# Dilated v blocks of 72 and 108 rows in a fused attention and gated unit kernel

## The chip, the cores and the metric

The kernel runs on one core of a Trainium2 chip. The metric is the time of one execution on the device in microseconds (us), as the median of several runs. A core has five engines that run side by side: TensorE (PE, matmuls and transposes into PSUM), VectorE (DVE), ScalarE (ACT), GpSimd (POOL) and SyncE (SP), which here issues the transfers. The transfers themselves are carried by 16 DMA engines[...].

## The reference, cut to what matters

Eight batches of eight heads, 576 positions, head size 64. Heads 0 to 3 use a plain window of 32 keys, heads 4 to 7 a dilated one: 32 keys at a distance of 4. The result goes through a causal convolution of 5 taps, a sigmoid gate and two 512 x 512 matmuls.

```python
rel = pos[:, None] - pos[None, :]
mask_plain = (rel >= 0) & (rel < window)                       # window = 32
mask_dil = (rel >= 0) & (rel < window * dilation) & (rel % dilation == 0)   # dilation = 4
...
attn = softmax(scale * q @ k.T, masked)      # heads 0-3 plain, heads 4-7 dilated
x = (attn @ v).transpose(0, 2, 1, 3).reshape(B, S, H * D)
...
gate_pre += conv_w[k] * xp[:, k:k + S, :]    # k = 0..4
gate = 1.0 / (1.0 + np.exp(-gate_pre))
out = (gate * (x @ w_val)) @ w_out
```

In the dilated heads a query at position 4t + r sees only keys at positions 4t' + r. The kernel therefore splits the 576 positions into four residues r with 144 places t each (TT), and a query at t sees keys t - 31 to t.

## The kernel before, in words

The work comes in 16 units: for each batch one unit of the four dilated heads and one of the four plain heads. For each unit, SP loads q and k (576 KB each) and v. TensorE transposes q and k into PSUM (line 431), DVE and ACT copy them to SBUF (lines 292 and 294), TensorE makes the scores (line 450), ACT takes the exponential (line 470), DVE multiplies by the mask (line 476), and TensorE multiplies with v (line 487 for dilated, 514 for plain heads). DVE divides by the sum (lines 497 and 526). After both units of a batch come the transposes of the result (lines 535 and 551), the convolution (line 569), the gate and the two big matmuls (lines 584 and 600), and the stores (line 614).

Of a plain unit, q and k pass through a cast on POOL (line 294, tiles qc and kc) before TensorE can transpose them; of a dilated unit they are transposed as loaded (tiles qn and kn). All v goes through a cast on POOL, from `va` to `vd` for dilated heads and from `vp` to `vpb` for plain ones.

The dilated v of a batch is cut into two blocks for the two halves of the queries, t = 0 to 71 (z = 0) and t = 72 to 143 (z = 1). Queries of the first half need keys 0 to 71, those of the second half keys 41 to 143. `KB` (line 219) is the number of partitions of each block's tile, 80 and 128. Block 1 puts key t on partition t - T1, with T1 = TT - 128 = 16. Its lowest partitions hold keys that no query of this half sees, so they are not loaded: `Z1` (line 221) is the first partition that is loaded, 16, and the partitions below it are set to zero once, at the start (line 364, on DVE). So block 0 loads keys 0 to 79 (80 rows, 320 KB), block 1 keys 32 to 143 (112 rows, 448 KB). A row is the four residues of one place t, that is 1 KB from each of four heads.

The matmul of line 487 uses `et[0:KB[z]]` and all KB[z] partitions of `vd`. The mask makes the weights of keys outside the window zero.

The order of the work is set before the program is built. A planner (`Plan`) holds a list of tasks with dependencies, costs and a due time (`KEY`), and places them on the engines; the tasks are then written out in the order of their planned starts. Loads all lie on SP's queue, one after the other, in the order of the units: for a dilated unit q, k, v block 0, v block 1, for a plain unit q, k, v half 0, v half 1. The planner's cost for the two dilated v loads is written out as 1.25 and 1.75. Every load waits until the tile that it writes has been read for the last time: there are two buffers each of va and vp, three of qn and kn, and three of vd and vpb. In the first 20 us, where the plan finds TensorE idle, it puts warm matmuls (line 627) whose result nobody reads.

The lines of the loads:

```python
rows = v[b, 4:8].rearrange("h (p r) d -> p h (r d)", r=R)
if z == 0:
    nc.sync.dma_start(out=vas[z][n % 2], in_=rows[0:KB[0]])             # line 401
else:
    nc.sync.dma_start(out=vas[z][n % 2][Z1:KB[1]], in_=rows[T1 + Z1:TT])  # line 403
```

Of the kernel before, what the change touches and what calls it, by code (L numbers as in the profile page):

```python
# [197 lines left out]
def kernel(  # L198
# [17 lines left out]
    W = 32  # L216
    TT = S // R
    QB = TT // 2
    KB = (80, 128)
    T1 = TT - KB[1]  # L220
    Z1 = 16
    JP, JD = 9, 18
    scale = 1.0 / float(D) ** 0.5
    NCH = Dm // 128
# [22 lines left out]
    vps = [consts.tile([128, 4 * NG, 2, D], FP32, name=f"vp{i}") for i in range(2)]  # L247
    vas = [[consts.tile([KB[z], 4, R * D], FP32, name=f"va{z}{i}") for i in range(2)]
           for z in range(2)]
    vds = [[consts.tile([KB[z], 2, R, DA], BF16, name=f"vd{z}{i}") for i in range(NVD)]  # L250
           for z in range(2)]
# [58 lines left out]
    def const(name, eng, dur, emit, deps=(), key=-50):  # L310
        return plan.add(name, key, {eng: (dur, dur + 0.05)}, lambda t: emit(), deps,
                        port=("POOL",))
# [42 lines left out]
    def dve_consts():  # L355
# [7 lines left out]
        for x in vas[1]:  # L363
            nc.vector.memset(x[0:Z1], 0.0)
    c_dv = const("dve_consts", "DVE", 2.2, dve_consts, key=-59)
# [31 lines left out]
    def load_vd(u, n, z):  # L397
        b = units[u][0]
        rows = v[b, 4:8].rearrange("h (p r) d -> p h (r d)", r=R)
        if z == 0:  # L400
            nc.sync.dma_start(out=vas[z][n % 2], in_=rows[0:KB[0]])
        else:
            nc.sync.dma_start(out=vas[z][n % 2][Z1:KB[1]], in_=rows[T1 + Z1:TT])

# [74 lines left out]
    def attn_d(t, sc, i, hf):  # L479
# [3 lines left out]
        for z in range(2):  # L483
            for x in range(2):
                for hh in range(2):
                    c = 2 * z + hh
                    nc.tensor.matmul(out=ps[:, x * 512 + c * DA:x * 512 + (c + 1) * DA],  # L487
                                     lhsT=et[0:KB[z], x, c * QB:c * QB + 128],
                                     rhs=vds[z][n][:, hh, 2 * hf + x, :],
# [396 lines left out]
```

## Time and profile before

| what | value |
|---|---|
| time, median of 3 runs | 193.21 us (190.97 to 197.29) |
| span of the profiled run | 191.4 us |
| mean granted TensorE clock | 0.988 |
| transfers | 43.41 MB, of these read from HBM 33.56 MB |

The busy shares of the engines are shares of the span. The row of tenths cuts the span into 40 slices of 4.8 us; a 9 means that the 16 DMA engines were busy 90% or more of the slice on the mean. The page's section on DMA issues gives each kind of transfer with its count, its size and the median time from issue to landing:

```profile
qn<-in_q_dram SPq DMA_DIRECT2D x16, 576.0 KB, 9.8
kn<-in_k_dram SPq DMA_DIRECT2D x16, 576.0 KB, 11.3
vp<-in_v_dram SPq DMA_DIRECT2D x15, 384.0 KB, 11.4
va<-in_v_dram SPq DMA_DIRECT2D x8, 448.0 KB, 9.9
va<-in_v_dram SPq DMA_DIRECT2D x8, 320.0 KB, 7.1
```

A landing time of about 10 us for a load of half a megabyte is mostly time spent queued behind earlier loads. In the list of groups a row gives line, engine and operation, the tiles and shapes, the count, then busy time and mean duration, then the idle time of the engine before them and what ended it. In a timeline, a row is start, length, engine, line, operation, tiles, count, and in brackets the idle time before it and who ended it.

### The profile page before, as it was taken

How to read it: one execution, taken by the hardware profiler on the slowest of the kernel's cores; microseconds unless marked ns; L12 is line 12 of the kernel's file. 1: busy time of each engine (PE TensorE's matmuls, PEld its weight loads, DVE VectorE, ACT ScalarE, POOL GpSimd, SP SyncE). 2: the span in 40 equal slices, each digit the busy share in tenths (PEclk: the TensorE clock that was granted, in tenths of full speed). 3: DMA queues.
4: the chain of work that ended last, by engine and by line, in shares of the span. 5: the costliest groups of instructions: out<-in, count | busy, mean ns of one | idle time of the engine just before them, and what ended most of it. 6: DMA issues, size and time to landing. Idle time of an engine off the chain costs nothing.

```text
span 191.4 us, 6733 instructions
## 1 busy us (share of the span) xinstructions
PE 166.2 (87%) x2892; PEld 113.2 (59%) x2892; DVE 128.4 (67%) x239; ACT 123.0 (64%) x204; POOL 61.7 (32%) x99
## 2 busy tenths in 40 slices
PE   7999988788888779989896998989999989999890
PEld 2546456655676547766673765655675876757540
DVE  7498585967576858667877576997667978930500
ACT  2448976575796839768845577775786394658151
POOL 7964308236332552803632207351007000000000
PEclk9999999999999999999999699999999999999998
DMA  5999999999999999999999839996451312035256
GB/s 199 269 384 235 379 255 288 234 264 278 232 341 335 252 290 233 366 294 303 296 210 269 245 115 259 361 246 247 169 172 52 113 58 110 3 104 160 68 169 215
DMA packets 32102, 43.41 MB, mean 227 GB/s; under 512 B 1877, under 2 KB 20293, under 8 KB 32074
## 3 DMA queue, kind: packets, MB, share of 16 engines
q1 hardware_dynamic: 32064, 42.99, 81.3%
q8 instruction: 22, 0.36, 0.9%
q14 instruction: 6, 0.05, 0.1%
q10 hardware_dynamic: 10, 0.01, 0.1%
HBM read 33.56 MB, written 9.44 MB: 225 GB/s over the span
## 4 chain that ended last, share of the span: by engine, by line
PE 57%; DVE 12%; ACT 11%; DMA 9%; issue 6%; POOL 1%; ACTq 0%; SPq 0%; DVEq 0%
PE ps L600 14%; PE ps L584 13%; DMA kn<-in_k_dram 8%; PE ps L569 7%; PE ps L627 6%; PE ps L431 5%; PE ps L450 4%; ACT et L470 4%; PE ps L487 3%; ACT osb L605 3%; DVE et L476 3%; PE ps L514 2%; PE ps L535 2%; DVE qT L294 2%; ACT qT L292 2%
## 5 line engine op out<-in xcount | busy, mean ns | idle before, releaser
L470 ACT ACTIVATE et<-ps 128x576 bf16<-128x576 f32 x64 | 40.6, 653 | 17.4 <-PE ps L450 17.2
L584 PE MATMUL ps<-xT,w_val 128*128 128x288 bf16 x256 | 36.0, 286 | 3.5 <-issue 2.2
L600 PE MATMUL ps<-w_out,gy 128*128 128x512 bf16 x144 | 35.7, 380 | 2.9 <-ACT osb L605 1.9
L593 DVE SCALAR_TENSOR_TENSOR gy<-gy,ps 128x576 bf16<-128x576 bf16 x32 | 23.9, 750 | 14.9 <-PE ps L584 14.7
L605 ACT ACTIVATE osb<-ps 128x512 f32<-128x512 f32 x35 | 20.0, 598 | 18.9 <-PE ps L600 17.0
L294 POOL CAST vd<-va 80x512 bf16<-80x512 f32 (+1 forms) x32 | 20.7, 678 | 33.1 <-DMA va<-in_v_dram 14.2
L584 PEld LDWEIGHTS <-w_val 128*128 128x128 bf16 x256 | 23.7, 98 | 11.2 <-issue 5.6
L569 PE MATMUL ps<-xT,diag 64*64 64x288 bf16 x640 | 25.1, 287 | 2.4 <-issue 0.7
L294 POOL CAST vpb<-vp 128x768 bf16<-128x768 f32 x16 | 13.5, 863 | 38.6 <-DMA vp<-in_v_dram 21.7
L476 DVE TENSOR_TENSOR et<-et,mask_p 128x576 bf16<-128x576 bf16 x32 | 18.7, 591 | 7.0 <-ACT et L470 6.3
L476 DVE TENSOR_TENSOR et<-et,mask_d 128x576 bf16<-128x576 bf16 x32 | 20.2, 636 | 4.3 <-ACT et L470 3.9
L497 DVE TENSOR_TENSOR xnd<-ps,rec 72x512 bf16<-72x512 f32 x32 | 22.0, 687 | 1.1
L600 PEld LDWEIGHTS <-gy 128*128 128x128 bf16 x144 | 12.7, 98 | 15.6 <-issue 3.1
L577 ACT ACTIVATE gy<-ps 128x576 bf16<-128x576 f32 x32 | 20.2, 658 | 2.7 <-PE ps L569 2.5
L569 PEld LDWEIGHTS <-diag 64*64 64x64 bf16 x640 | 18.0, 107 | 5.3 <-issue 3.4
L292 ACT COPY xT<-ps 128x576 bf16<-128x576 bf16 (+1 forms) x20 | 15.7, 786 | 7.2 <-PE ps L551 3.7
L292 ACT COPY qT<-ps 128x576 bf16<-128x576 bf16 x22 | 13.6, 643 | 10.5 <-PE ps L431 7.8
L450 PE MATMUL ps<-qT,kT 64*64 64x96 bf16 (+1 forms) x640 | 18.6, 203 | 1.6 <-ACT kT L292 1.0
L450 PEld LDWEIGHTS <-kT 64*64 64x64 bf16 (+1 forms) x640 | 12.4, 102 | 12.3 <-issue 8.1
L627 PE MATMUL ps<-warm 128*128 128x512 bf16 x52 | 15.7, 429 | 1.3 <-DVE warm L314 1.3
L292 ACT COPY kT<-ps 128x576 bf16<-128x576 bf16 x21 | 12.9, 644 | 4.6 <-PE ps L431 2.7
L526 DVE TENSOR_TENSOR xnp<-ps,den 96x768 bf16<-96x768 f32 x16 | 15.3, 954 | 0.5
(68 smaller groups left out, 181.1 us busy)
## 6 DMA issues: line engine op xcount, KB each, us to landing
qn<-in_q_dram SPq DMA_DIRECT2D x16, 576.0 KB, 9.8
kn<-in_k_dram SPq DMA_DIRECT2D x16, 576.0 KB, 11.3
out_dram<-osb SPq DMA_DIRECT2D x24, 256.0 KB, 2.6
vp<-in_v_dram SPq DMA_DIRECT2D x15, 384.0 KB, 11.4
va<-in_v_dram SPq DMA_DIRECT2D x8, 448.0 KB, 9.9
va<-in_v_dram SPq DMA_DIRECT2D x8, 320.0 KB, 7.1
out_dram<-osb SPq DMA_DIRECT2D x8, 192.0 KB, 2.4
wst<-in_moe_w_val_dram SPq DMA_DIRECT2D x2, 512.0 KB, 8.4
```

What stands on the lines that cost most here:

```text
L292: nc.scalar.copy(out=dst, in_=src)
L294: op(t.eng).tensor_copy(dst, src)
L450: nc.tensor.matmul(out=ps[po:po + pn, x, out_c:out_c + ln], lhsT=kw[rb, k0:k0 + (pn - 1) * kstep + 1:kstep], rhs=qT[rb, q0:q0 + (ln - 1) * ...
L470: nc.scalar.activation(out=ets[(2 * i + hf) % NE][:, :, 0:HALF], in_=ps[:, :, 0:HALF], func=AF.Exp, scale=scale)
L476: op(t.eng).tensor_tensor(out=ev, in0=ev, in1=m.to_broadcast([128, 2, HALF]), op=ALU.mult)
L497: nc.vector.tensor_tensor(out=xnd[i % 2][:, 4 * hf:4 * hf + 4].rearrange("p (x j) h d -> p x (j h) d", x=2), in0=av[:, :, :, 0:D], in1=rec ...
L569: nc.tensor.matmul(out=ps[o:o + 64, 512 * f:512 * f + HALF], lhsT=diag[lo:lo + 64, c * K + kk, :], rhs=xT[lo:lo + 64, b % NX, c, f * HALF ...
L584: nc.tensor.matmul(out=ps[:, 512 * f:512 * f + HALF], lhsT=w_val[f][:, mc, c * 128:(c + 1) * 128], rhs=xT[:, b % NX, mc, K - 1 + f * HALF: ...
L593: nc.vector.scalar_tensor_tensor(out=y, in0=y, scalar=1.0, in1=ps[:, :, 0:HALF], op0=ALU.add, op1=ALU.mult)
L600: nc.tensor.matmul(out=ps, lhsT=y[:, c, 128 * n:128 * n + 128], rhs=w_out[f][:, c, :], start=(c == 0), stop=(c == NCH - 1))
L605: nc.scalar.activation(out=osb[z % NO], in_=bank(ou), func=AF.Copy, scale=0.5)
L627: plan.idle = lambda t: nc.tensor.matmul(out=bank(t), lhsT=warm[:, 0:128], rhs=warm, start=True, stop=True)
```

## The change

Block 0 gets a tile of 72 partitions instead of 80 and loads keys 0 to 71, exactly those that its queries see. Block 1 is loaded from partition 20 on instead of 16, that is keys 36 to 143; partitions 0 to 19 are zeroed at the start. The two loads of a batch shrink from 320 and 448 KB to 288 and 432 KB. The casts of block 0, the memsets of its column of ones and the matmuls of line 487 for z = 0 go over 72 partitions instead of 80. The aim is not to load rows that no query uses. The order of the instructions on every engine is the same as before.

```diff
-    KB = (80, 128)
+    KB = (72, 128)
     T1 = TT - KB[1]
-    Z1 = 16
+    Z1 = 20
```

## The prediction

> **What bounds the kernel now.** I read the busy slices first, then the DMA queues, then the order in time of the loads, of the casts on POOL and of TensorE's transposes, because the diff touches loads alone. From the page:
>
> ```profile
> span 191.4 us, 6733 instructions
> PE 166.2 (87%) x2892; PEld 113.2 (59%) x2892; DVE 128.4 (67%) x239; ACT 123.0 (64%) x204; POOL 61.7 (32%) x99
> DMA  5999999999999999999999839996451312035256
> DMA packets 32102, 43.41 MB, mean 227 GB/s; under 512 B 1877, under 2 KB 20293, under 8 KB 32074
> q10 hardware_dynamic: 10, 0.01, 0.1%
> ```
>
> TensorE is the busiest engine, but the DMA row is at 9 from the second slice to the 23rd (a slice is 4.8 us, so from 5 to 110 us). Both look like a bound; the question is who waits for whom, and when. The timeline of POOL's casts, and beside it that of TensorE:
>
> ```profile
> 10.29 2.28 POOL L294 CAST vd<-va 80x512 bf16<-80x512 f32 x4
> 28.97 1.18 POOL L294 CAST vd<-va 80x512 bf16<-80x512 f32 x2 [7.22 <-DMA va<-in_v_dram]
> 30.76 1.40 POOL L294 CAST vd<-va 128x512 bf16<-128x512 f32 x2 [0.61 <-DMA va<-in_v_dram]
> 35.37 1.15 POOL L294 CAST kc<-kn 128x1152 bf16<-128x1152 f32 x1 [1.90 <-DMA kn<-in_k_dram]
> 50.59 1.15 POOL L294 CAST kc<-kn 128x1152 bf16<-128x1152 f32 x1 [1.99 <-DMA kn<-in_k_dram]
> 67.00 1.15 POOL L294 CAST kc<-kn 128x1152 bf16<-128x1152 f32 x1 [1.72 <-DMA kn<-in_k_dram]
> ```
> ```profile
> 27.76 0.62 PE L431 MATMUL ps<-ident_b,kn 128*128 128x128 bf16 x8 [0.73 <-DMA kn<-in_k_dram]
> 36.58 0.68 PE L431 MATMUL ps<-ident_b,kc 128*128 128x128 bf16 x9 [1.05 <-POOL kc L294]
> 52.29 0.66 PE L431 MATMUL ps<-ident_b,kc 128*128 128x128 bf16 x9 [0.73 <-ACT qT L292]
> 74.11 0.66 PE L431 MATMUL ps<-ident_b,kc 128*128 128x128 bf16 x9
> ```
>
> The reader is to see the slack between a load and TensorE's use of it (start plus length of the cast, against the start of the transposes). At 27.76 TensorE starts when kn lands: slack 0. At 36.58 it starts 0.06 us after the cast that began at 35.37: slack 0. At 52.29 the cast has been done since 51.74: slack 0.55. At 74.11 the cast has been done since 68.15: slack 6.0. So up to about 52 us the loads set TensorE's pace; after that TensorE falls behind the loads and they have room to spare, although the DMA row still shows 9. The chain of waits says the same: its only long DMA step is kn, and none of the loads appears on it after 36 us.
>
> [...] conv_nat has 5 rows, and its queue q10 shows 10 packets, 5 rows and 5 completions. The page lists 117 issues on SP; 117 x 16 + 5 = 1877, which is exactly the count under 512 B. So every load from SP now uses 16 engines. [...] The trace does not show single engines. [...] Between 22 and 24 us, where 128-row k is loaded, DMA moves 409 GB/s; between 16 and 18, where the 64-row halves of vp are loaded, 231; in the v stretch:
>
> ```profile
> GB/s 237 310 218 319 182 510 182 182 182 300 218 164 164 200 182 146 319 146 164 200 200 237 246 200 182 219 109 182 219 209 218 218 237 127 200 164 182 218 237 218
> DMA packets 454, 0.48 MB, mean 214 GB/s; under 512 B 17, under 2 KB 448, under 8 KB 453
> ```
>
> (window 24.75 to 27.00 us).
>
> **The change part by part.** Rows: (80 - 72) + (112 - 108) = 12 rows of 4 KB fewer per head group, 48 KB; over 8 pairs of loads 0.39 of 43.41 MB. At the 214 GB/s above that would be 0.22 us less per pair, if nothing else changed.
>
> Engines: [...] both loads go from 16 engines to 12. A row is four pieces of 1 KB (one per head). Per engine, before: 80 x 4 / 16 + 112 x 4 / 16 = 20 + 28 = 48 pieces; after, on twelve: 72 x 4 / 12 + 108 x 4 / 12 = 24 + 36 = 60, on the other four none. Twelve engines get 12 pieces more per pair. Price of a piece: in the v stretch 431 pieces (448 less 17 completions) on 16 engines in 2.25 us make 84 ns each[...]. The lower end is from the stretch 12 to 14 us, where 340 pieces of 2304 B make 2 x 16 / 340 = 94 ns each, 24.5 GB/s per engine, hence an estimate of 42 ns for 1 KB. So 12 pieces cost 0.5 to 1.0 us. I take 0.8 to 1.0[...]. The pair takes about 3.0 us now (from kn at 27.76 to the cast of the second block at 30.76).
>
> Who feels it: the loads form one stream on SP's queue, with qp, kp, vp, qd, kd behind each pair, so each pair makes all later loads that much later. At 27.76 one pair lies ahead (its casts ran at 10.29): +0.8 to 1.0. At 36.58 two: +1.6 to 2.0. At 52.29 three: +2.4 to 3.0, less the slack of 0.55, so TensorE is 1.9 to 2.5 us late, of which 1.6 to 2.0 were already there. Later pairs cost nothing: by 67 us four pairs make 3.2 to 4.0 us of lag, TensorE is itself some 2 us late, and 2 us are taken from a slack of 6. TensorE's order is fixed and it is 87% busy, so the 2 us are not won back. Sum: +1.9 to +2.5 us, middle 2.2; 193.2 + 2.2 = 195.4.
>
> Costed at nothing: POOL's casts, 668 ns with 80 rows and 688 with 128, so rows are not what they cost; the attention matmuls, 195 ns with 80 rows and 193 with 128; the two memsets of 16 or 20 rows on DVE, 912 ns each, which take as long on more partitions and run at 3 to 5 us while TensorE issues warm matmuls. No wait and no instruction is added, and the planner's costs for these loads (1.25 and 1.75) are constants, so the order on every engine stays.
>
> **The rivals.**
> (a) [...] engines don't matter[...]. Against: 60 pieces at even the unhindered 42 ns are 2.5 us, so twelve engines cannot do better than that, and the measured 3.0 leaves room only if waits shrink. With three pairs saving up to 0.22 us each: 192.6 to 193.2.
> (b) Worse. The twelve engines stay out of step with the four, which run ahead into the next transfers; these land only when the last engine is done[...]. With a lag of 1.5 to 2.2 us per pair: 3 x 1.5 - 0.55 = 4.0 to 3 x 2.2 - 0.55 = 6.1 us, so 197 to 199.5. For it: load stretches already fall from 409 to about 210 GB/s. [...]
> (c) Fewer engines than twelve[...]: 8 and 4 would give 36 + 108 = 144 pieces per engine, at 42 ns 6.0 us per pair, 3 more than now; 3 x 3 - 0.55 = 8.5, and 201.7 or more. [...]
> (d) Faster. The loads give back what TensorE waits for them at 27.76 and 36.58, 1.8 us: 191.4. It needs the v loads to become shorter by more than the 48 KB.
>
> **How the numbers follow.** Forecast 0.52, (a) 0.15, (b) 0.25, (c) 0.04, (d) 0.04. The bound of 2% is 3.9 us, 197.1. Slower: (b), (c) and a fifth of the forecast for spread between runs (190.97 to 197.29 before): 0.39. Faster over 2% needs more than (d) gives, with spread: 0.06. The rest, 0.55, is within 2%. The range runs from (a) to the top of (b): 192.8 to 199.8.
>
> **What would show it.** Engines: under 512 B must read 101 x 16 + 16 x 12 + 5 = 1813, and packets in all 32102 - 384 - 64 = 31654; 1877 would mean that 16 engines are still used and the engine step is wrong. Lag: kc's casts now at 35.37 and 50.59 should start 1.6 to 2.0 and 2.4 to 3.0 us later, and TensorE's wait before them should grow. The cast at 67.00 should move too without TensorE waiting for it. If the casts have moved and the end has not, TensorE won the time back[...]. A wait for va or kn behind TensorE after 60 us would mean that the slack of 6 us was spent, and (b).

## The result, and the profile after

The changed kernel takes 200.35 us (median of 4 runs, 199.81 to 202.28); the kernel before took 193.33 us beside it (190.97 to 197.29). The ratio is 1.0423 with a 95% interval of 1.0297 to 1.0550: slower, by about 7 us, three times the 2.2 us that were forecast and above the range. Ratios here and below are of the runs within 1.5% of the fastest run of their kernel; where none is given, too few of those were left or only one run was made, and the times stand by themselves.

The head of the page of the kernel after, with the row of granted clock:

```profile
span 198.7 us, 6733 instructions
PE 169.3 (85%) x2892; PEld 114.3 (58%) x2892; DVE 128.8 (65%) x239; ACT 122.6 (62%) x204; POOL 60.9 (31%) x99
...
PEclk9999999969988996999999999999999999999998
DMA  6999999999999999999999999999976211115256
...
DMA packets 31654, 43.02 MB, mean 217 GB/s; under 512 B 1813, under 2 KB 19845, under 8 KB 31626
```

The same instructions as before, and 0.39 MB less to move. The DMA row is at 9 up to the 29th slice (144 us) where it was at 9 up to the 23rd (110 us): fewer bytes, and the DMA engines are busy with them for longer. Under 512 B stands 1813 and the packets are 31654, the two counts that the prediction named for twelve engines.

When the loads land is seen in the timeline of POOL, in the casts of the plain unit's k (start, length, tiles, and in brackets POOL's idle time before it and who ended it):

```profile
18.50 1.15 POOL L294 CAST kc<-kn 128x1152 bf16<-128x1152 f32 x1 [2.21 <-DMA kn<-in_k_dram]
...
38.17 1.15 POOL L294 CAST kc<-kn 128x1152 bf16<-128x1152 f32 x1 [1.69 <-DMA kn<-in_k_dram]
...
56.64 1.15 POOL L294 CAST kc<-kn 128x1152 bf16<-128x1152 f32 x1 [2.75 <-DMA kn<-in_k_dram]
...
76.15 1.15 POOL L294 CAST kc<-kn 128x1152 bf16<-128x1152 f32 x1 [2.10 <-DMA kn<-in_k_dram]
...
114.28 1.15 POOL L294 CAST kc<-kn 128x1152 bf16<-128x1152 f32 x1 [2.29 <-DMA kn<-in_k_dram]
```

Before, these five began at 16.64, 35.37, 50.59, 67.00 and 98.47 us, and the one between the last two at 80.26 (after: 92.30). The first and the last of them, before:

```profile
16.64 1.15 POOL L294 CAST kc<-kn 128x1152 bf16<-128x1152 f32 x1 [1.34 <-DMA kn<-in_k_dram]
...
98.47 1.15 POOL L294 CAST kc<-kn 128x1152 bf16<-128x1152 f32 x1 [2.19 <-DMA kn<-in_k_dram]
```

The lag is 1.86, 2.80, 6.05, 9.15, 12.04 and 15.81 us: six pairs of loads, 2.6 us for each on the mean. TensorE's transposes of the same tile, from its timeline:

```profile
39.38 0.68 PE L431 MATMUL ps<-ident_b,kc 128*128 128x128 bf16 x9 [1.92 <-POOL kc L294]
...
57.84 1.14 PE L431 MATMUL ps<-ident_b,kc 128*128 128x128 bf16 x9 [2.36 <-POOL kc L294]
...
82.38 0.66 PE L431 MATMUL ps<-ident_b,kc 128*128 128x128 bf16 x9
...
120.90 0.66 PE L431 MATMUL ps<-ident_b,kc 128*128 128x128 bf16 x9
```

These were at 36.58, 52.29, 74.11 and 112.73 before. The last of them, before:

```profile
112.73 0.66 PE L431 MATMUL ps<-ident_b,kc 128*128 128x128 bf16 x9
```

TensorE is 2.80, 5.55, 8.27 and 8.17 us later, and 7.3 at the end of the span. At the first two the cast has just ended and TensorE was idle for it, 1.92 and 2.36 us (1.05 us before the first of them in the kernel before, and before the second it waited for ACT). At the last two there is no bracket: TensorE did not wait, though the casts were 9 and 15.8 us late. So the loads set the pace up to 58 us, which explains 5.55 of the 7.3 us. The last 1.8 us came later, and not from a wait for a load: between the second and the third of these transposes TensorE loses another 2.7 us, part of which it wins back by the end. In that stretch the clock is granted at half for 3.4 us twice, at 57.7 (which is why nine transposes took 1.14 us at 57.84) and at 74.8; an earlier such stretch is at 40.6. And one idle time that no record explains, ahead of line 584, is 3.56 us (at 74.72) where it was 2.23 before (at 68.01). These two were not told apart. The stretch at 74.8 begins right behind the idle time of 3.56 us; near the first two, TensorE's waits last 1.92 and 2.36 us. What sets off such a stretch was not shown.

The DMA engines' share and the bytes moved, in two windows of 20 us of each kernel (columns: window, length, busy time and count of PE, PEld, DVE, ACT, POOL, granted clock, DMA share, GB/s). Before:

```profile
20.00:40.00 20.00, 16.45 (x317) 11.36 (x307) 14.09 (x25) 13.84 (x23) 7.91 (x10) 1.00 1.09 296
40.00:60.00 20.00, 17.34 (x366) 12.27 (x367) 14.61 (x30) 15.10 (x25) 8.19 (x11) 1.00 1.09 286
```

After:

```profile
20.00:40.00 20.00, 15.97 (x300) 10.69 (x299) 13.35 (x22) 13.30 (x22) 6.66 (x8) 1.00 1.06 267
40.00:60.00 20.00, 16.45 (x284) 11.09 (x284) 11.90 (x22) 13.10 (x22) 6.47 (x8) 0.86 1.06 227
```

The DMA share stays above 1 (the records of pieces overlap) while GB/s falls from 286 to 227. So the queues hold work all the time, and each piece takes longer: over the whole trace the mean record of a 2304-byte piece (the plain units' q and k, queued right behind the v pair) grew from 121 to 149 ns, of a 4608-byte piece (the dilated q and k) from 243 to 262, while the 1 KB pieces of the v pair itself went only from 67 to 68. The pieces that slowed down are not those of the changed loads but their neighbours'.

The trace also holds the time at which each DMA engine reports the end of its part of a load, one end for each engine (no view prints these): 16 for each load of q, twelve for each changed load of v beside one record at its issue. For the plain q of the second batch, issued at 20.37 us right behind the v pair, the first four of 16 ends come from 27.15 to 27.83 us and the other twelve from 33.52 to 35.27. So four engines are 5.7 us ahead of the rest: they have finished even the first half of the plain v, two loads further on, at 33.13. In the kernel before, the 16 ends of the same q lie between 29.93 and 32.09, and no two neighbours are as much as 1 us apart. Whether this lead is the cause, is what the experiments ask.

### The profile page after: what moved, and what is told of

It reads as the page before. It is cut to its first block, busy times and chain, and to the rows that moved or that the text cites. A ratio compares the mean times of both kernels' runs of the same rounds, so it can differ in the third digit from the quotient of the medians.

```text
span 198.7 us, 6733 instructions
## 1 busy us (share of the span) xinstructions
PE 169.3 (85%) x2892; PEld 114.3 (58%) x2892; DVE 128.8 (65%) x239; ACT 122.6 (62%) x204; POOL 60.9 (31%) x99
## 2 busy tenths in 40 slices
DMA packets 31654, 43.02 MB, mean 217 GB/s; under 512 B 1813, under 2 KB 19845, under 8 KB 31626
## 4 chain that ended last, share of the span: by engine, by line
PE 46%; DMA 24%; ACT 10%; DVE 7%; issue 6%; SPq 2%; POOL 2%; ACTq 0%; DVEq 0%
DMA kn<-in_k_dram 23%; PE ps L584 14%; PE ps L600 12%; PE ps L569 5%; PE ps L431 4%; PE ps L450 4%; ACT osb L605 3%; ACT et L470 3%; PE ps L514 2%; PE ps L487 2%; PE ps L535 2%; DVE et L476 2%; DVE qT L294 2%; POOL kc L294 2%; ACT kT L292 2%
## 5 line engine op out<-in xcount | busy, mean ns | idle before, releaser
L470 ACT ACTIVATE et<-ps 128x576 bf16<-128x576 f32 x64 | 40.6, 653 | 22.0 <-PE ps L450 21.7
L584 PE MATMUL ps<-xT,w_val 128*128 128x288 bf16 x256 | 38.2, 297 | 4.4 <-issue 3.6
L584 PEld LDWEIGHTS <-w_val 128*128 128x128 bf16 x256 | 24.5, 101 | 13.2 <-issue 6.5
L294 POOL CAST vd<-va 72x512 bf16<-72x512 f32 (+1 forms) x32 | 20.0, 652 | 37.6 <-DMA va<-in_v_dram 36.1
L627 PE MATMUL ps<-warm 128*128 128x512 bf16 x52 | 16.2, 438 | 1.3 <-DVE warm L314 1.3
```

The lines of the kernel that those rows point to most:

```text
L294: op(t.eng).tensor_copy(dst, src)
L470: nc.scalar.activation(out=ets[(2 * i + hf) % NE][:, :, 0:HALF], in_=ps[:, :, 0:HALF], func=AF.Exp, scale=scale)
L584: nc.tensor.matmul(out=ps[:, 512 * f:512 * f + HALF], lhsT=w_val[f][:, mc, c * 128:(c + 1) * 128], rhs=xT[:, b % NX, mc, K - 1 + f * HALF: ...
```

## The experiments

Four theories. A: the twelve engines simply have more to do (60 pieces for 48 in each pair). B: the four engines without a share run ahead into later transfers, so that pieces of different transfers meet and slow each other. C: it is the rows themselves (72 and 108, or where they start). D: the harm is done inside the pair, beside the q and k in flight at its start.

**Same rows, nearly all engines (e1_split).** Each load is cut into a part that divides by 16 and a remainder.

```diff
-    KB = (80, 128)
+    KB = (72, 128)
-    Z1 = 16
+    Z1 = 20
-            nc.sync.dma_start(out=vas[z][n % 2], in_=rows[0:KB[0]])
+            nc.sync.dma_start(out=vas[z][n % 2][0:64], in_=rows[0:64])
+            nc.sync.dma_start(out=vas[z][n % 2][64:72], in_=rows[64:72])
-            nc.sync.dma_start(out=vas[z][n % 2][Z1:KB[1]], in_=rows[T1 + Z1:TT])
+            nc.sync.dma_start(out=vas[z][n % 2][32:128], in_=rows[T1 + 32:TT])
+            nc.sync.dma_start(out=vas[z][n % 2][20:32], in_=rows[T1 + 20:T1 + 32])
```

> The rows of the change (72 and 108), but block 0 loaded as 64 + 8 rows and block 1 as 96 + 12, so that most rows go over all 16 engines: at most 48 pieces of 1 KB per engine and pair of loads, as before, at least 40; 16 transfers more in all. Theory A (the transfer waits for its busiest engine: the twelve engines have 60 pieces instead of 48): back to 193 to 194.5 us, and the casts of kc at 35 and 51 us again. Theory B (engines that get no share of the pair run ahead[...]): nearly back as well, 193.5 to 195, since the shares differ by 8 pieces and not by 60. Theory C (it is the rows: casts, memsets, matmuls on 72 rows, or where block 1 begins): stays at 199 to 202.

Measured: 188.63 us (188.09 to 189.50) beside 192.72 of the kernel before, ratio 0.9842 (0.9755 to 0.9929). POOL's timeline of it:

```profile
35.79 1.15 POOL L294 CAST kc<-kn 128x1152 bf16<-128x1152 f32 x1 [2.57 <-DMA kn<-in_k_dram]
51.89 1.36 POOL L294 CAST kc<-kn 128x1152 bf16<-128x1152 f32 x1 [2.66 <-DMA kn<-in_k_dram]
```

The second and third cast are back within 0.4 and 1.3 us of where they were before, and the loss is gone. Under 512 B stands 2037, 160 more than before: 52 for each batch, which fits parts of 64, 8, 96 and 12 rows on 16, 8, 16 and 12 engines, where the two loads of before had 32. The bytes, the partitions and the matmuls over 72 partitions are those of the changed kernel, so C falls: the loss does not come from the rows. (Whether it is truly faster than before is taken up below.)

**One engine without a share instead of four (e2_k15).** Blocks of 75 and 105 rows on fifteen engines (the count is below): 20 + 28 = 48 pieces for each, as many as sixteen got before.

```diff
-    KB = (80, 128)
+    KB = (75, 128)
-    Z1 = 16
+    Z1 = 23
```

> Blocks of 75 and 105 rows (second block from partition 23), both multiples of 15: 75 x 4 / 15 + 105 x 4 / 15 = 20 + 28 = 48 pieces on 15 engines, none on the sixteenth. Theory A: the busiest engine has the 48 pieces of before, so 193 to 194.5 us. Theory B: one engine of 16 runs ahead by 48 pieces per pair, so something between, 194.5 to 198. If the rows alone mattered (C), near the 200 of the change, as both blocks are within 3 rows of it.

Measured: 191.76 us (187.57 to 196.24) beside 192.72. Under 512 B stands 1861, that is 16 less than before: fifteen engines in each of the 16 loads. B had asked for 194.5 to 198, so it missed here. The lead is there all the same: one end of the plain q comes 3.4 us ahead of the other fifteen in the second batch and 5.4 us in the third, but the third cast of k stands at 49.30, no later than before. A lead of one engine is not harmful as such; the spread leaves a small cost open.

**Each block alone (e3_block0, e4_block1).**

```diff
-    KB = (80, 128)
+    KB = (72, 128)     # e3_block0 alone
-    Z1 = 16
+    Z1 = 20            # e4_block1 alone
```

> Only block 0 changed: 72 rows on 12 engines, block 1 with 112 rows on 16. Busiest engine 24 + 28 = 52 pieces. Theory A: 4 of the 12 extra pieces, so a third of the 7.0 us: about 195.7. Theory B: the four engines are 24 pieces ahead per pair instead of 60, so 40 percent: 196.2[...].

> Only block 1 changed: 108 rows on 12 engines, block 0 with 80 rows on 16. Busiest engine 20 + 36 = 56 pieces. Theory A: 8 of the 12 extra pieces, two thirds of the 7.0 us: about 198. Theory B: the four engines are 36 pieces ahead per pair instead of 60: 197.5, or more. The two halves should sum to the whole change if neither has a threshold.

Measured: block 0 alone 197.77 us (195.20 to 198.54), ratio 1.0232 (1.0068 to 1.0396), casts of k at 39.78 and 58.32; block 1 alone 201.41 us (197.37 to 202.01), casts at 40.80 and 57.92, beside 192.72. Against the medians that is +5.0 and +8.7, and both together made +7. Under A the two parts, 4 and 8 pieces more on the busiest engine, should add up to the whole, about a third and two thirds of it. The medians do not do that, but the runs of each kernel spread over 3 to 5 us, so the times do not settle it. The third cast is 7.7 and 7.3 us later than before, where both blocks together made it 6.05 us later; that speaks against A, but the two profiled runs are the slowest of their kernels (198.54 and 202.01 us). So it is likely, and not shown, that one uneven load in each batch is enough for most of the harm. Nor is it known why the two parts would not add up. The lead does have a bound: in the trace of the changed kernel each of SP's 109 transfers from the ninth on is issued after the last end of the transfer eight before it (the plain k of the second batch at 22.85 us, that end at 22.78). But with block 0 alone the four engines were only 1.5 and 2.2 us ahead at the plain q of the second and third batch, well inside this bound.

**The stream of loads alone (s_full16, s_full12).** Everything but the loads is taken out: in eight rounds q, k, both v blocks, then q, k and both v halves of the plain unit, in the kernel's order (which differs in the last batch alone, where the kernel has the plain unit first) and buffers, with small copies on POOL as readers, and stores of zeros. One with the rows of before, one with the change.

```diff
-    KB = (80, 128)     # s_full12 alone
+    KB = (72, 128)
-    Z1 = 16
+    Z1 = 20
...
+    for b in range(B):     # both kernels
+        u = 2 * b
+        load_q(u, "q"); load_q(u, "k")
+        load_vd(u, b, 0)
+        load_vd(u, b, 1)
+        load_q(u + 1, "q"); load_q(u + 1, "k")
+        load_vp(u + 1, b, 0)
+        load_vp(u + 1, b, 1)
```

> Only the loads of q, k and v of all 16 units, in the order of the units (dilated first in every batch), in the same buffers, with blocks of 80 and 112 rows; of each load one column is read by POOL; all arithmetic is left out, and zeros are stored at the end. It measures the stream of loads by itself. Expected: about 15 us per batch, as between the casts of kc before, if compute did not hold the loads up.

> The same loads-only kernel with blocks of 72 and 108 rows on 12 engines. Theory A: 12 pieces of 1 KB at 42 to 84 ns more per batch, 0.5 to 1.0 us, so 4 to 8 us over the eight batches, and the four engines simply idle. Theory B: 2 to 3 us per batch, 16 to 24 us in all, as in the changed kernel, and slower pieces of 2304 and 4608 B too. If the slowdown came from the feedback of compute (buffers freed later), the two loads-only kernels would differ by under 0.5 us per batch.

Measured: 143.13 us with 80 and 112 rows, 171.19 with 72 and 108. Timeline of POOL, the reader of the first and of the eighth dilated q, of the kernel with 16 engines:

```profile
4.65 0.18 POOL L434 COPY seen<-qn 128x1 f32<-128x1 f32 x1 [4.21 <-DMA qn<-in_q_dram]
...
100.50 0.18 POOL L434 COPY seen<-qn 128x1 f32<-128x1 f32 x1 [2.11 <-DMA qn<-in_q_dram]
```

and with twelve:

```profile
4.74 0.18 POOL L434 COPY seen<-qn 128x1 f32<-128x1 f32 x1 [4.29 <-DMA qn<-in_q_dram]
...
127.73 0.18 POOL L434 COPY seen<-qn 128x1 f32<-128x1 f32 x1 [2.56 <-DMA qn<-in_q_dram]
```

Seven rounds take 95.85 and 122.99 us: 13.69 us each with sixteen engines and 17.57 with twelve. That is 3.88 us lost in each round, without TensorE, without any other work on the core, and with less to load. A window in the middle of each (columns: window, length, busy time of DVE and POOL, clock, DMA share, GB/s), first sixteen engines:

```profile
45.00:96.00 51.00, 0.00 (x0) 4.80 (x26) 1.00 1.11 288
```

and twelve:

```profile
45.00:96.00 51.00, 0.00 (x0) 3.88 (x21) 1.00 1.01 232
```

The DMA share falls by a tenth, the bytes moved by a fifth. Pieces of 2304 bytes take 167 ns for 115, of 4608 bytes 260 for 217.

**The pair alone (s_v16, s_v12).** The same with only the two dilated v loads in each round.

```diff
-        load_q(u, "q"); load_q(u, "k")
         load_vd(u, b, 0)
         load_vd(u, b, 1)
-        load_q(u + 1, "q"); load_q(u + 1, "k")
-        load_vp(u + 1, b, 0)
-        load_vp(u + 1, b, 1)
```

> Only the dilated v loads, 80 and 112 rows, back to back over eight batches with two buffers each, nothing of q, k or the plain v; zeros stored at the end; all arithmetic is left out. It measures the pair by itself: [...] 3.0 us (as in the whole kernel) per pair.

> The same with 72 and 108 rows on 12 engines. Theory A: 0.5 to 1.0 us more per pair. Theory B: the pair alone has no other transfers to collide with, so here too only 0.3 to 1.0 us more; most of the 3 us per batch of the changed kernel should be missing here.

Measured: 57.87 and 57.15 us, stores included. POOL's reader of the second block in the first and in the seventh pair, sixteen engines first:

```profile
6.05 0.18 POOL L432 COPY seen<-va 64x1 f32<-64x1 f32 x1 [1.60 <-DMA va<-in_v_dram]
...
24.02 0.18 POOL L432 COPY seen<-va 64x1 f32<-64x1 f32 x1 [1.51 <-DMA va<-in_v_dram]
```

and twelve:

```profile
5.82 0.18 POOL L432 COPY seen<-va 64x1 f32<-64x1 f32 x1 [0.94 <-DMA va<-in_v_dram]
...
22.70 0.18 POOL L432 COPY seen<-va 64x1 f32<-64x1 f32 x1 [1.34 <-DMA va<-in_v_dram]
```

Six pairs took 17.97 and 16.88 us: 3.00 us for a pair on sixteen engines, 2.81 on twelve. The windows over the loads, sixteen engines first:

```profile
5.00:25.00 20.00, 0.00 (x0) 2.38 (x13) 1.00 1.10 268
```

and twelve:

```profile
5.00:25.00 20.00, 0.00 (x0) 2.56 (x14) 1.00 0.87 283
```

With a quarter of the engines idle (share 0.87 for 1.10) more bytes are moved, as each 1 KB piece takes 50 ns instead of 66. Here A falls as a cause by itself: the pair with the twelve extra pieces, which the prediction priced at 0.5 to 1.0 us, is 0.2 us shorter (B had allowed 0.3 to 1.0 us more, which did not come either). And the 3.88 us lost in a round of the whole stream are more than the 2.81 us that the pair takes by itself.

**A barrier behind the pair (s_bar16, s_bar12).** In the stream of loads, the plain unit's q and k now wait until both v blocks have landed, so that no engine can run from the pair into them. The wait is made by a copy from the v tiles into the tiles that those loads write.

```diff
-        nc.gpsimd.tensor_copy(seen[0:KB[0], 0:1], vas[0][b % 2][:, 0, 0:1])
-        nc.gpsimd.tensor_copy(seen[64:128, 1:2], vas[1][b % 2][64:128, 0, 0:1])
+        nc.gpsimd.tensor_copy(kns[(u + 1) % NQ][0:KB[0], 0:1], vas[0][b % 2][:, 0, 0:1])
+        nc.gpsimd.tensor_copy(qns[(u + 1) % NQ][64:128, 0:1], vas[1][b % 2][64:128, 0, 0:1])
         load_q(u + 1, "q"); load_q(u + 1, "k")
```

> The loads-only kernel with blocks of 80 and 112 rows, and a barrier: the plain q load of each batch, and all that stands behind it on SP's queue, is issued only when both dilated v blocks have landed (POOL copies one column of them into the tiles of that q and k first). All arithmetic is left out. The barrier costs an empty stretch per batch; it is the base for the next kernel: 13.1 us per batch plus some 2 us, about 155 to 165 us in all.

> The same barrier with 72 and 108 rows on 12 engines. Theory B (the harm comes from the four engines that run ahead into the next transfers, past the pair): they cannot run ahead any more, so the 28 us between the two loads-only kernels shrink to under 5 us, and the pieces of 2304 B cost the same in both. Theory D (the harm is in the pair itself beside whatever lies ahead of it, q and k, or in the smaller number of engines): the difference stays at 20 us or more.

Measured: 159.51 us with sixteen engines, 157.91 with twelve. The pages' DMA lines, sixteen engines:

```profile
DMA packets 27394, 40.91 MB, mean 259 GB/s; under 512 B 1296, under 2 KB 19712, under 8 KB 27392
```

and twelve:

```profile
DMA packets 26946, 40.51 MB, mean 259 GB/s; under 512 B 1232, under 2 KB 19264, under 8 KB 26944
```

The difference of 28 us is gone (now -1.6), both move 259 GB/s, and 2304-byte pieces take 110 ns in both. Against the streams without it, the barrier costs sixteen engines 16 us and saves twelve 13 (single runs, on different chips). The lead is gone too: of the 16 ends of a plain q, no two neighbours are more than 0.3 us apart with the barrier on twelve engines, and up to 7.4 us without it. D falls with it: the q and k ahead of the pair still run beside it, and nothing is lost. What costs is what the four engines do once they are past the pair: B.

**Whom they meet (s_nvp16, s_nvp12).** The stream of loads without the plain v, which goes to 64 partitions in 512-byte pieces.

```diff
         load_q(u + 1, "q"); load_q(u + 1, "k")
-        load_vp(u + 1, b, 0)
-        load_vp(u + 1, b, 1)
```

> The loads-only kernel without the loads of the plain v (q, k, dilated v in two blocks, q, k per batch), blocks of 80 and 112 rows. All arithmetic is left out. Base for the next: 13.1 less 3.3 us per batch, so some 26 us less than the 141 of the full stream: 113 to 118.

> The same with 72 and 108 rows on 12 engines. If the leading engines do harm by meeting the 64-row loads of the plain v, the difference to the 16-engine stream falls from 28 us to under 8. If the v pair beside the 128-row loads of q and k is enough, it stays at 15 us or more, and pieces of 2304 B still cost 140 ns or more against 115.

Measured: 108.22 and 116.99 us, so 8.8 us remain of 28, just over the 8 that were expected; a round takes 9.12 and 10.41 us (readers of q at 4.83 and 68.65, and at 4.71 and 77.57). Two thirds of the harm need the plain v in the stream. The 2304-byte pieces of the plain q and k grow from 105 to 123 ns without it and from 115 to 167 with it. In the changed kernel the four engines are indeed at the 64-row halves of v while the twelve are still at the plain q and k: in the second batch four ends of the first half come by 33.13 us, the twelve late ends of q from 33.52 on. Why pieces that meet there take longer was not shown.

**The half clock (e_warm).** The changed kernel with 6, 8 and 10 warm matmuls ahead of the k transposes of units 1, 3 and 5, to fill TensorE's idle time there.

```diff
         ps = pair(t).bitcast(BF16)
+        for _ in range({1: 6, 3: 8, 5: 10}.get(u, 0) if name == "k" else 0):
+            nc.tensor.matmul(out=pair(t)[:, 0:512], lhsT=warm[:, 0:128], rhs=warm, start=True, stop=True)
```

> The changed kernel with 6, 8 and 10 more warm matmuls on TensorE just ahead of the transposes of kc in units 1, 3 and 5, where it waits 1.4, 1.9 and 2.4 us for the load. They should fit into the waits. If the halved clock windows that follow these waits in the changed kernel (at 40.6 and 57.7 us) are caused by the waits, the two are gone and the time falls by up to 2 us, to 198 to 200; the lag of the casts stays. If the clock plays no part in the 7 us, the time stays at 200 to 202.

Measured: 203.42 us (200.30 to 206.75), ratio 1.0489 (1.0376 to 1.0602) to the kernel before. The windows of half clock did not go away but moved, to 19.0, 56.5 (6.8 us long), 77.0 and 135.0, and the ten warm matmuls took 3.34 us where they met one. These ten did not even fall into the wait: they began at 61.24 us, when the cast that they were to bridge (59.68 to 60.83) had ended, and so held the transposes up. The run says nothing on how much of the last 1.8 us the clock has; that stays open.

**Is a split better than either kernel? (e_split80, e_split_again, e_split104).** The split of e1_split on the rows of before (64 + 16 and 96 + 16); e1_split again in more rounds on another chip; and 72 and 104 rows, split in 64 + 8 and 96 + 8.

```diff
-    KB = (80, 128)     # e_split104 alone; e_split80 keeps both lines
+    KB = (72, 128)
-    Z1 = 16
+    Z1 = 24
-            nc.sync.dma_start(out=vas[z][n % 2], in_=rows[0:KB[0]])
+            nc.sync.dma_start(out=vas[z][n % 2][0:64], in_=rows[0:64])
+            nc.sync.dma_start(out=vas[z][n % 2][64:KB[0]], in_=rows[64:KB[0]])
-            nc.sync.dma_start(out=vas[z][n % 2][Z1:KB[1]], in_=rows[T1 + Z1:TT])
+            nc.sync.dma_start(out=vas[z][n % 2][32:128], in_=rows[T1 + 32:TT])
+            nc.sync.dma_start(out=vas[z][n % 2][Z1:32], in_=rows[T1 + Z1:T1 + 32])
```

> The rows of the kernel before (80 and 112), but each load in two: 64 + 16 and 96 + 16 rows, all on 16 engines. It asks why the split kernel with 72 and 108 rows was faster than before. If the 48 KB less per batch did it: the time of before, 191 to 195. If the splitting did it [...]: 188 to 190.

> The split kernel once more (72 rows as 64 + 8, 108 as 96 + 12). If its gain over before is real: 187.5 to 190, ratio 0.975 to 0.99. If it was the spread between runs: 191 to 194.

> As the split kernel, with block 1 from partition 24 on, keys 40 to 143: 104 rows as 96 + 8, block 0 as 64 + 8. 16 KB less per batch and at most 48 pieces per engine, as before. If fewer bytes help at all: 187 to 189.5; it differs from the split kernel by less than 1 us in any case.

Measured: e_split80 190.10 us beside 192.46, ratio 0.9896 (0.9815 to 0.9977), between its two expectations. e_split_again 193.86 us (190.93 to 195.72, 16 runs) beside 193.34 (189.07 to 196.96, 21 runs), ratio 1.0136 (1.0070 to 1.0201). e_split104 192.83 us, ratio 1.0107 (1.0004 to 1.0210). The 1.6% that e1_split won on one chip, in four runs, did not come again on another: there the ratio is above 1, and the medians of all runs are 0.3% apart. So by these ratios a split stands within 2% of the kernel before: it takes away the harm, and no gain from the 12 rows fewer in each batch holds on both chips. No version that beats both kernels was found.

## Why the prediction was wrong, point by point

- **The engines: right.** Twelve for both loads, with both counts of packets exact. Ahead of the result the twelve were the author's estimate; the counts under 512 B show them: 80 and 112 rows on 16 engines (1877), 72 and 108 on twelve (1813), 75 and 105 on fifteen (1861). Single engines, which the prediction said the trace does not show, can be told apart in it after all, by the 16 ends of a load.
- **The slack: right.** After 58 us TensorE waits for no load, though the casts fall behind by 9.15 us at the cast once at 67.00 and by 15.81 at the sixth. TensorE, itself 8 us late, needs each load 8 us later, which adds to the 6.0 us of slack; so the wait that was named as the sign of (b), after 60 us, did not come, although (b)'s cause was at work.
- **The lag for each pair: the step that failed.** "So 12 pieces cost 0.5 to 1.0 us. I take 0.8 to 1.0". Two and three pairs were to make 1.6 to 2.0 and 2.4 to 3.0 us; they made 2.80 and 6.05, and the stream of loads alone loses 3.88 in each round. Its size and its cause were both off. The extra pieces by themselves cost nothing: 3.00 to 2.81 us for the pair alone, 159.51 to 157.91 us for the stream with the barrier. What costs is the lead of the four engines. That the cost would lie at the upper end, 0.8 to 1.0, was the author's estimate. What a piece takes depends on its neighbours as well: a 1 KB piece takes 50 ns instead of 66 in the pair alone and 56 instead of 66 with the barrier, but 68 instead of 67 in the whole kernel. So in the kernel twelve more pieces can still be some 0.8 us of the lag (an estimate, 12 x 68 ns); that the four engines ahead keep these pieces from getting shorter is likely, but no run shows it.
- **Rival (b): the right mechanism, and about the right price for the loads.** At 1.5 to 2.2 us per pair it gave 197 to 199.5. The barrier shows that the harm comes from engines that run past the pair, as (b) had it. With the lag of three pairs as measured, 6.05 us or 2.0 for each, its own sum gives 193.2 + 6.05 - 0.55 = 198.7: the loads' part, in its range. The rest to 200.35 is about the 1.8 us after 58 us (with the half clock and the idle time before line 584 as candidates), which no step held. The barrier run, with the same loads to the same partitions and no lead, shows no lag at all (157.91 us on twelve engines, 159.51 on sixteen). Why pieces of different transfers slow each other was not shown.
- **Rivals (a), (c), (d): out.** (a) and (d) have no lag of the casts; (c) would show other counts.
- **Costed at nothing: right, as far as 2% can show.** e1_split and e_split_again keep the casts, matmuls and memsets of 72 partitions and stand within 2% of before.

## What to carry to other kernels

In a busy stream, look at how many engines each transfer gets. Here 6% fewer bytes in the v loads, on twelve engines instead of sixteen, cost the kernel 4%. The same bytes in split loads, a multiple of 16 rows and a small remainder, stayed within 2% of the kernel before, and loads on fifteen engines cost nothing that could be measured. Judge a transfer in the stream that it is part of: alone this pair got shorter, and in the stream its neighbours paid. Where several engines share one queue of transfers, ask of every load on fewer engines what the others do meanwhile, and what they will meet there.

## What was not expected of the hardware

- The v pair by itself is no slower on twelve engines than on sixteen (2.81 and 3.00 us), since each 1 KB piece takes 50 ns instead of 66.
- Four engines that run ahead take 288 GB/s to 232 in a stream of loads alone, with all other work gone; a barrier in that stream, which costs 16 us where the engines keep step, saves 13 where they don't.
- One engine that ran 3.4 and 5.4 us ahead of fifteen made no load later; four that ran 5.7 us ahead of twelve did. How far ahead is not the measure by itself.
- One and the same split kernel stood at 0.984 of the kernel before on one chip, in four runs, and with it by the medians of all runs (193.86 and 193.34 us) on another: a gain of 1.5% on one chip is not yet one of the kernel.
